# Seven half-width products for two groups of the third block of an attention and SwiGLU kernel

## The chip, the cores and the metric

The kernel runs on one core of one Trainium2 chip. The metric is the device time of one execution in microseconds (us), as the median of several runs. Five engines work side by side: TensorE (PE in the profile) multiplies matrices, VectorE (DVE) and ScalarE (ACT) read its results out of PSUM and do elementwise work, GpSimd (POOL) does elementwise work in SBUF, and SyncE (SP) here issues nearly all DMA transfers. Each engine runs its instructions in order; they wait for each other through semaphores.

## The reference, cut to what matters

```python
# q, k, v: (8, 12, 448, 64); g_q, g_k: (64,)
q_n, k_n = (rmsnorm(q, g_q), rmsnorm(k, g_k))
scores = scale * np.matmul(q_n, k_n.transpose(0, 1, 3, 2))
attn = softmax(scores)                       # over the keys
x = np.matmul(attn, v)                       # -> (3584, 768) tokens by features
g = x @ w_gate                               # (768, 1536), float64 weights
val = x @ w_val
out = (silu(g) * val) @ w_out                # (1536, 768)
```

All results are float32.

## The kernel before, in words

The 8 sequences are worked on in four blocks of two (`block(n)`, n = 0 to 3; in words the first to the fourth). A block has an **up phase** (`x @ w_gate`, `x @ w_val` and the gating) and a **down phase** (the product with `w_out`). The attention of the next block's twelve head pairs (`attention(m)`) is woven into the down phase; its first pairs begin before the up phase has ended. The last block has no attention beside it.

The products work on 3 x 3 arrangements of blocks, with 15 sums of blocks on either side and one product for each: the weights are turned once, at the start, into 15 sums and single blocks of 128 x 128 for each piece (`convert`; kept in device memory as `up_sides[g]` and `down_sides`; `UP_SUMS` is the order of the 11 sums, `BLOCKS` that of the four plain blocks), the activations into 15 sums in `xs` (`sides`), and each product is added to running results t0 to t5 and d by ACT and DVE (`UP_READ`). The up phase falls into four **groups** g = 0 to 3 of hidden features. An ordinary group has 15 steps for the gate and 15 for the value, each one product (`up_product`, line L1498) of two matmuls of 128 x 128 by 128 x 448, since the contraction has two chunks c. Its weights come in three pieces of five steps (`up_load`, `load_sides`, line L1448) into a ring `ws` of two entries.

A group can also be computed by **sevens** (`sevens`, line L1752). There the 2 x 2 scheme of gate and value, two chunks and two halves of the 448 tokens is done in seven products of half width (224 columns) instead of eight. It needs four differences of weights and, on the token side, four differences S1 to S4 of halves for each of the 15 sums. POOL makes the latter while group 0's first pass runs (`halves_of`, L1640); one of them overwrites half of `xs` and is undone afterwards (`restore`, L1654). S1, S2 and S4 lie in `hs`, in the attention's `t`/`QT`/`KT` region of the buffer `work`, and in `es` (the ring `e`); the keys `held` keep the attention out of these for as long. The seven products run as four streams: X and Y, and two products later (`LAG`) Z and W. POOL adds the streams' results (L1863, L1881), DVE joins the last parts, ACT applies SiLU (L1901), DVE multiplies (L1905). With sevens in a block, group 0 runs as two passes with the sevens between them (`passes`): gate, then the sevens, then value, then any further ordinary groups. Before the change only the fourth block (n = 3) has such groups: 1, 2 and 3.

The weight differences are made ahead of time by `prepare`, 15 pieces for three groups, a piece for three of the 15 products (index u): SP loads the six operand blocks' rows from `up_sides` (L1941), POOL makes four subtractions (L1955), and SP stores to `up7_g` (L1962). `PREPARE` gives each block its pieces and `PREPARE_PACE` the spacing of their due times. Before the change there are 8 pieces in the second block (n = 1) and 7 in the third (n = 2), in two places in turn (`es` and the end of `work`), and all seven left operands are stored, plain ones among them. In the fourth block each load of a stream (L1707) is then one DMA from `up7`: four matrices for X and Y, in three places in turn, three for Z and W, in two.

The order on every engine is written by a planner (`Order`): each piece of work has an engine, an estimated cost, a due time, a list of pieces it follows and the rings it takes or uses; it is run through once when the program is built, and the instructions are emitted in that order. The rings are named buffers with a fixed number of entries (`BUFS`): `ws` 2, `qk` 4, `e` 4, `t` 2 and so on.

Of the kernel before, what the change touches and what calls it, by code (L numbers as in the profile page):

```python
# [493 lines left out]
def fast(  # L494
# [91 lines left out]
    def take(name, key, shape):  # L586
# [46 lines left out]
    UP_SUMS = (8, 7, 1, 13, 10, 14, 3, 11, 4, 0, 5)  # L633
# [117 lines left out]
    def attention(m):  # L751
# [19 lines left out]
        def load(x, src):  # L771
            def emit():
# [18 lines left out]
                after=[staged.get(PAIRS)],  # L791
# [622 lines left out]
    PREPARE, PREPARE_PACE, up7_done = {1: [(g, u) for g in (1, 2, 3) for u in range(5)][:8], 2: [(g, u) for g in (1, 2, 3) for u in range(5)][8:]}, 16.0, {}  # L1414
# [44 lines left out]
    def block(n):  # L1459
# [15 lines left out]
        def up_product(g, step, x, which, load, key, when, flip, alone):  # L1475
# [117 lines left out]
        def up_load(g, piece, which, when):  # L1593
            key, more = ("ws", (n, g, piece, which)), []
            if which is not None and piece == (0 if which else 2 if len(seven) % 2 == 0 else None):
                key, more = (("qk", (n, g, piece, i)) for i in range(1)), [("qk", (n, g, piece, i)) for i in range(1, 3)]
                key = next(key)
# [11 lines left out]
            users[key] = [key, *more]  # L1609
            last_load[:] = [load]  # L1610
# [58 lines left out]
        def sevens(begin_seven):  # L1669
# [18 lines left out]
            for (k, late), times in sorted(pieces.items(), key=lambda of: of[1][0]):  # L1688
# [4 lines left out]
                else:  # L1693
                    at = (k - count + 2) % 3
                    name = f"xy{at}"
                    base, tile_of = (0, [ws_keys[at]]) if at < 2 else (4 * P, qk_keys)
# [4 lines left out]
                def load(key=key, tile_of=tile_of, late=late, base=base, k=k, opens=opens):  # L1701
# [7 lines left out]
                done = order.add(  # L1709
                    "SP", 0.6, times[0] - 12.0, load,  # L1710
                    after=[*last_load, up7_done[seven[k // 5], k % 5], clusters[EARLY * (n + 1) - 1, "total"]],
                    takes=[key] + tile_of * opens, uses=tile_of * (not opens),
                    moves=[transfer(P, (36 if late else 48) * P)],
                    early=10.0, rank=SIDES_RANK,
                )
                last_load[:] = [done]
# [11 lines left out]
            for when, stream, j, i in steps:  # L1728
# [64 lines left out]
                def tile_at(stream, t, g=g, key_of=key_of):  # L1793
# [4 lines left out]
                    if ends and key_of(stream, t) == qk_keys[-1]:  # L1798
                        return work[:, 0:S]
# [24 lines left out]
                def emit_read(stream=stream, t=t, how=how, x=x, ps=ps, value=value, first=first, tile_at=tile_at, g=g):  # L1824
# [9 lines left out]
                extra = [("wl", (n, g))] if stream == "W" and x == 4 else []  # L1834
                done = order.add(
                    "ACT" if how == COPY else "DVE", (0.36 if stream == "W" else 0.53) if how == COPY else us,
                    when + 0.2, emit_read, after=[last, *before], takes=extra or ([value] if first else []),
                    uses=([value] if value and not first else []) + ([bank_tile] if bank_tile else []), rank=60.0,
# [159 lines left out]
        if n in PREPARE:  # L1998
            prepare()
# [276 lines left out]
```

## Time and profile before

| | |
|---|---|
| median of 3 runs | 1446.1 us (1443.5 to 1447.08) |
| the profiled execution's own time | 1448.08 us |
| its span, first to last instruction | 1446.2 us |
| granted TensorE clock | 0.997 of full speed |
| PE busy | 1412.9 us (98%) |
| DVE, ACT, POOL busy | 927.0 (64%), 612.5 (42%), 581.1 us (40%) |
| up phase of n = 1 | 483.66 to 669.60 us: 185.94 us |
| up phase of n = 2 | 832.11 to 1018.14 us: 186.03 us |
| up phase of n = 3 | 1179.67 to 1347.01 us: 167.34 us |
| DMA | 234.65 MB, mean 162 GB/s |

Times in the trace are counted from the span's start. A row of an engine's timeline or of the chain gives start, duration and the work (engine, line, output and inputs by their names, a count). A group row gives line, engine, operation, names, shapes and count, then busy time and mean duration, then the idle time before it with what ended it. A float32 matmul appears as two records of PE, which overlap, so the time of a product is read from the distance between starts and not from the sum of durations. The time of a DMA to its landing counts from its issue. Names in the trace are those of the buffers: `work` holds `qk`, `t`, `QT` and `KT`; `mm` and `at` are the banks of the ordinary products; `st` holds the streams Z and W, among others; `up` is the tensor `up7`.

### The profile page before, as it was taken

What the parts mean: (1) busy time and instruction counts of PE and PEld (TensorE: products, weight loads), DVE (VectorE), ACT (ScalarE), POOL (GpSimd) and SP (SyncE); (2) the same over time, 40 slices, a digit from 0 to 9 for tenths busy, and PEclk for the clock granted to TensorE, in tenths of its full rate; (3) what the DMA queues carried; (4) which work ended last, traced back from release to release, by engine and by line L of the source; (5) the groups of instructions that cost most, each with busy time, mean ns of one, the idle gap of its engine ahead of it and who ended that gap; (6) DMA issues with size and microseconds to landing.
All of it is one profiled execution on the core that took longest, in us unless ns stands there. A gap on an engine that the chain in (4) does not pass through costs nothing.

```text
span 1446.2 us, 20499 instructions
## 1 busy us (share of the span) xinstructions
PE 1412.9 (98%) x7006; PEld 739.1 (51%) x7006; DVE 927.0 (64%) x1566; ACT 612.5 (42%) x1244; POOL 581.1 (40%) x698
## 2 busy tenths in 40 slices
PE   8999999989999999999999999999999999999997
PEld 3455454434444455544444455544444448997553
DVE  5889876887866444346776633355686753777633
ACT  6875444466553221256645222245555412432200
POOL 3756666635453122213444222312244448677000
PEclk9999999999999999999999999999999999999999
DMA  7777989854634666843444467673355354543335
GB/s 197 211 217 263 356 279 292 263 164 92 124 78 97 181 228 219 241 138 91 108 91 103 104 195 257 209 188 91 80 110 111 88 119 154 177 168 110 97 100 101
DMA packets 422182, 234.65 MB, mean 162 GB/s; under 512 B 281396, under 2 KB 399924, under 8 KB 420148
## 3 DMA queue, kind: packets, MB, share of 16 engines
q1 hardware_dynamic: 410800, 231.87, 57.3%
q10 hardware_dynamic: 11140, 1.38, 0.7%
q8 instruction: 57, 0.93, 0.3%
q14 instruction: 57, 0.47, 0.1%
q0 software_dynamic: 128, 0.00, 0.0%
HBM read 177.93 MB, written 55.25 MB: 161 GB/s over the span
## 4 chain that ended last, share of the span: by engine, by line
PE 84%; DMA 4%; DVE 4%; SPq 3%; ACT 2%; issue 1%; POOL 1%; ACTq 0%; POOLq 0%; DVEq 0%
PE mm L2076 21%; PE mm L1498 21%; PE at L1498 19%; PE at L1064 7%; PE st L985 7%; PE st L1752 3%; PE at L1752 2%; PE mm L1752 2%; SPq L783 2%; DMA work<-in_k_dram 2%; PE st L1095 1%; PE mm L1095 1%; DMA out_dram<-spare 1%; ACT es L1000 1%; DMA work<-in_q_dram 1%
## 5 line engine op out<-in xcount | busy, mean ns | idle before, releaser
L1498 PE MATMUL mm<-xs,ws 128*128 128x448 f32 x820 | 340.0, 542 | 0.5 <-POOL sums L1863 0.3
L1498 PE MATMUL at<-xs,ws 128*128 128x448 f32 x720 | 301.3, 541 | 4.7 <-DVE v L1429 3.6
L1498 PEld LDWEIGHTS mm<-xs,ws 128*128 128x128 f32 x820 | 155.9, 191 | 154.7 <-issue 150.9
L1498 PEld LDWEIGHTS at<-xs,ws 128*128 128x128 f32 x720 | 135.7, 190 | 142.4 <-issue 124.0
L2076 PE MATMUL mm<-gt,ws 128*128 128x448 f32 x448 | 175.5, 543 | 0.0
L903 POOL TENSOR_TENSOR work<-work,rr 128x448 f32<-128x448 f32 x72 | 72.5, 1026 | 231.4 <-DVE rr L730 82.4
L985 PE MATMUL st<-work 64*64 64x448 f32 (+1 forms) x1536 | 151.4, 500 | 11.8 <-ACT work L933 4.9
L1000 ACT ACTIVATE es<-st 128x896 f32<-128x896 f32 x129 | 114.3, 914 | 100.7 <-PE at L1064 85.7
L2076 PE MATMUL mm<-hs,ws 128*128 128x448 f32 x384 | 151.4, 545 | 0.0
L1005 POOL TENSOR_TENSOR sums<-es 128x896 f32<-128x896 f32 x36 | 76.5, 2126 | 158.4 <-PE st L1095 83.9
L2076 PEld LDWEIGHTS mm<-gt,ws 128*128 128x128 f32 x448 | 83.6, 190 | 83.0 <-issue 80.8
L1427 DVE TENSOR_TENSOR gt<-gt,mm 128x448 f32<-128x448 f32 x52 | 32.3, 621 | 134.5 <-PE mm L1498 132.7
L2076 PEld LDWEIGHTS mm<-hs,ws 128*128 128x128 f32 x384 | 71.2, 190 | 71.4 <-issue 69.9
L1064 PE MATMUL at<-es,v 64*64 64x448 f32 (+1 forms) x1032 | 106.2, 508 | 0.0
L1575 ACT ACTIVATE st<-gt 128x448 f32<-128x448 f32 x78 | 42.6, 547 | 129.3 <-DVE gt L1431 63.3
L985 PEld LDWEIGHTS st<-work 64*64 64x64 f32 x1536 | 50.5, 132 | 81.7 <-issue 36.6
L1425 ACT COPY gt<-mm 128x448 f32<-128x448 f32 x65 | 34.6, 532 | 122.8 <-PE mm L1498 122.7
L1955 POOL TENSOR_TENSOR es<-es 128x384 f32<-128x384 f32 x32 | 31.2, 998 | 121.7 <-DMA es<-up_sides 121.1
L1005 POOL TENSOR_TENSOR sums<-sums,es 128x896 f32<-128x896 f32 x36 | 75.4, 2094 | 2.8
L1064 PEld LDWEIGHTS at<-es,v 64*64 64x64 f32 (+1 forms) x1032 | 43.9, 133 | 56.6 <-issue 49.4
L1425 ACT COPY v<-at 128x448 f32<-128x448 f32 x74 | 39.4, 532 | 58.2 <-PE at L1498 56.7
L822 ACT ACTIVATE work<-work 128x448 f32<-128x448 f32 (+1 forms) x92 | 52.3, 584 | 22.9 <-DMA work<-in_k_dram 10.3
(263 smaller groups left out, 2144.9 us busy)
## 6 DMA issues: line engine op xcount, KB each, us to landing
ws<-up_sides SPq DMA_DIRECT2D x24, 1024.0 KB, 6.5
ws<-down_sides SPq DMA_DIRECT2D x16, 1024.0 KB, 5.7
ws<-down_sides SPq DMA_DIRECT2D x28, 512.0 KB, 5.0
up<-es SPq DMA_DIRECT2D x8, 1344.0 KB, 8.3
out_dram<-spare SPq DMA_DIRECT2D x168, 56.0 KB, 2.1
up<-work SPq DMA_DIRECT2D x7, 1344.0 KB, 9.2
v<-in_v_dram SPq DMA_DIRECT2D x96, 96.0 KB, 2.6
ws<-up_sides SPq DMA_DIRECT2D x12, 768.0 KB, 5.0
```

The lines of the kernel that those rows point to most:

```text
L822: nc.scalar.activation(tiles["t", m][:, x], of, AF.Square)
L903: nc.gpsimd.tensor_tensor(out=tiles["t", m][:, x], in0=tiles["qk", (m, x)], in1=rr.to_broadcast([P, NC, C]), op=ALU.mult,)
L985: nc.tensor.matmul(st[ds(D * x, D), h, 0:n], tiles["KT", m][rows, ds(P * j + D * of_keys, D)], tiles["QT", m][rows, ds(Q * of_queries, n)] ...
L1000: nc.scalar.activation(e, tiles["st", (m, j)][:, :, 0 : S * width(j) // P], AF.Exp)
L1005: nc.gpsimd.tensor_tensor(out=to, in0=tiles["e", (m, 0)] if j == 1 else to, in1=e, op=ALU.add)
L1064: nc.tensor.matmul(tiles["at", (m, x)][ds(D * h, D), ds(0, Q) if early else queries], tiles["v", m][rows, j, h], tiles["e", (m, j)][rows, ...
L1425: nc.scalar.copy(to, ps)
L1427: nc.vector.tensor_tensor(out=to, in0=old, in1=ps, op=ALU.add)
L1498: nc.tensor.matmul(ps(), w[:, 0 if alone else which, c, at], xs[:, SLOT[x], c], start=fresh and c == 0, stop=c == NC2 - 1, skip_group_chec ...
L1575: nc.scalar.activation(take(*act, [P, 2, TB])[:, 0, 0:S], to, AF.Silu)
L1752: nc.tensor.matmul(half(ps(), side), w[:, slot, at], part_of(of, x), start=fresh and side == 0, stop=True, skip_group_check=True,)
L2076: nc.tensor.matmul(banks[bank_of[s]][:, 0:S], w[:, s, g, at], where[x][:, g], start=fresh and i == 0, stop=i == NG - 1, skip_group_check=True,
```

## The change

Groups 1 and 2 of the third block (n = 2) are computed by sevens too, between group 0's two passes; group 3 follows there as an ordinary group.

All 15 pieces of differences are made in the second block (n = 1), due every 7.8 us instead of 16, in three places in turn: `es`, the end of `work`, and group 3's part of `gt`. That group's first results in n = 1 wait until the last piece there is stored (`gt_free`). Only the four differences of a piece are stored; the plain blocks are read from `up_sides` where they are needed, so a load for X and Y is one plain matrix and three differences and one for Z and W two plain ones and one difference, each as two or three DMAs. `prepare` is called ahead of the passes instead of behind them.

In the ring `qk`, a piece of group 0's first pass takes all four entries where the number of groups by sevens is even; the second pass's first piece takes three, and a fourth entry is taken by an empty piece ("places"), which the loads of the next block's q and k follow. These weights and those of the third X and Y place now begin at the start of `work`. In `UP_SUMS`, 4 and 11 change places.

```diff
-    UP_SUMS = (8, 7, 1, 13, 10, 14, 3, 11, 4, 0, 5)
+    UP_SUMS = (8, 7, 1, 13, 10, 14, 3, 4, 11, 0, 5)
...
-    SEVEN = {3: (1, 2, 3)}
+    SEVEN = {2: (1, 2), 3: (1, 2, 3)}
...
-        g: dram.tile([P, 5, 7, 3, P], F32, name=f"up7_{g}")
+        g: dram.tile([P, 5, 4, 3, P], F32, name=f"up7_{g}")
...
-                after=[staged.get(PAIRS)],
+                after=[staged.get(PAIRS), clusters.get("places")],
...
-    PREPARE, PREPARE_PACE, up7_done = {1: [...][:8], 2: [...][8:]}, 16.0, {}
+    PREPARE, PREPARE_PACE, up7_done = {1: [(g, u) for g in (1, 2, 3) for u in range(5)]}, 7.8, {}
...
-            tiles[key] = work[:, 4 * P :]
+            tiles[key] = work[:, 0 : 12 * P]
...
+            if which == 0 and (how == COPY or result == 2) and g == NG - 1:
+                before = gt_free
...
-                key, more = (("qk", (n, g, piece, i)) for i in range(1)), [("qk", (n, g, piece, i)) for i in range(1, 3)]
-                key = next(key)
+                key, *more = (("qk", (n, g, piece, i)) for i in range(3 if which else 4))
...
+            if more and which and n < NB - 1:
+                clusters["places"] = add(
+                    "SP", 0.0, when + 8.0, lambda: None, after=[load], takes=[("qk", (n, "rest", 0))],
+                )
...
-                    src = up7[seven[k // 5]][:, k % 5, 4:7] if late else up7[seven[k // 5]][:, k % 5, 0:4]
-                    nc.sync.dma_start(tiles[key], src.rearrange("p w x f -> p (w x f)"))
+                    first, plain = int(not late), 2 if late else 1
+                    here_of, i = up_sides[seven[k // 5]][:, 0:plain, int(late)], 0
...
+                            nc.sync.dma_start(
+                                w[:, 0:plain, ds(i * P, size * P)],
+                                here_of[:, :, ds(begin + here[0], size)].rearrange("p a x f -> p a (x f)"),
+                            )
...
+                    src = up7[seven[k // 5]][:, k % 5, 3:4] if late else up7[seven[k // 5]][:, k % 5, 0:3]
+                    nc.sync.dma_start(
+                        w[:, 2:3] if late else w[:, 1:4], src.rearrange("p w x f -> p w (x f)")
+                    )
...
-                    after=[*last_load, up7_done[seven[k // 5], k % 5], clusters[EARLY * (n + 1) - 1, "total"]],
+                    after=[last_load[0 if len(loads) > 4 else -1], up7_done[seven[k // 5], k % 5], clusters[EARLY * (n + 1) - 1, "total"]],
...
-            buffers = [(flat_es, ("e",)), (work[:, 2 * NJ * 2 * D * 2 :], ("t", "QT"))]
+            buffers = [
+                (flat_es, ("e",)), (work[:, 2 * NJ * 2 * D * 2 :], ("t", "QT")),
+                (gt[:, NG - 1].rearrange("p k t -> p (k t)"), ()),
+            ]
...
-                which = j % 2
+                which = (j + 1) % 3
...
-                for i, (to, one, two) in enumerate(((2, 1, 0), (3, 5, 2), (1, 5, 1), (6, 4, 3))):
+                for i, (to, one, two) in enumerate(((2, 1, 0), (3, 5, 2), (1, 5, 1), (4, 4, 3))):
...
-                        up7[g][:, u].rearrange("p w x f -> p (w x f)"), raw.rearrange("p w f -> p (w f)")
+                        up7[g][:, u].rearrange("p w x f -> p (w x f)"), raw[:, 1:5].rearrange("p w f -> p (w f)")
...
+            gt_free[:] = [emptied[2]]
+
+        gt_free = [None]
+        if n in PREPARE:
+            prepare()
         passes = [(g, (0, 1)) for g in range(NG) if g not in seven]
...
-        if n in PREPARE:
-            prepare()
```

More of the change, by code (lines that the diff above doesn't have):

```diff
@@ L1705, in load @@
                     tiles[key] = room[:, base : base + (9 if late else 12) * P]
-                    src = up7[seven[k // 5]][:, k % 5, 4:7] if late else up7[seven[k // 5]][:, k % 5, 0:4]
-                    nc.sync.dma_start(tiles[key], src.rearrange("p w x f -> p (w x f)"))
+                    w = tiles[key].rearrange("p (w f) -> p w f", f=3 * P)
+                    first, plain = int(not late), 2 if late else 1
+                    here_of, i = up_sides[seven[k // 5]][:, 0:plain, int(late)], 0
+                    part = UP_ORDER[3 * (k % 5) :][:3]
+                    for names, begin in ((UP_SUMS, 0), (BLOCKS, len(UP_SUMS))):
+                        here = sorted(names.index(x) for x in part if x in names)
+                        if here:
+                            size = len(here)
+                            nc.sync.dma_start(
+                                w[:, 0:plain, ds(i * P, size * P)],
+                                here_of[:, :, ds(begin + here[0], size)].rearrange("p a x f -> p a (x f)"),
+                            )
+                            i += size
+                    src = up7[seven[k // 5]][:, k % 5, 3:4] if late else up7[seven[k // 5]][:, k % 5, 0:3]
+                    nc.sync.dma_start(
+                        w[:, 2:3] if late else w[:, 1:4], src.rearrange("p w x f -> p w (x f)")
+                    )
                 done = order.add(
-                    "SP", 0.6, times[0] - 12.0, load,
-                    after=[*last_load, up7_done[seven[k // 5], k % 5], clusters[EARLY * (n + 1) - 1, "total"]],
+                    "SP", 1.4, times[0] - 12.0, load,
+                    after=[last_load[0 if len(loads) > 4 else -1], up7_done[seven[k // 5], k % 5], clusters[EARLY * (n + 1) - 1, "total"]],
                     takes=[key] + tile_of * opens, uses=tile_of * (not opens),
-                    moves=[transfer(P, (36 if late else 48) * P)],
+                    moves=[
+                        *(transfer((2 if late else 1) * P, 4 * P * i) for i in groups(UP_ORDER[3 * (k % 5) :][:3], UP_SUMS)),
+                        transfer(P, (12 if late else 36) * P),
+                    ],
                     early=10.0, rank=SIDES_RANK,
                 )
-                last_load[:] = [done]
+                last_load[:] = [last_load[-1], done]
                 loads[k, late] = done, key, tile_of
@@ L1834, in sevens @@
                 extra = [("wl", (n, g))] if stream == "W" and x == 4 else []
+                also = held[0:4] if extra else []
                 done = order.add(
@@ L1837, in sevens @@
                     when + 0.2, emit_read, after=[last, *before], takes=extra or ([value] if first else []),
-                    uses=([value] if value and not first else []) + ([bank_tile] if bank_tile else []), rank=60.0,
+                    uses=also + ([value] if value and not first else []) + ([bank_tile] if bank_tile else []), rank=60.0,
                 )
@@ L1895, in sevens @@
                     done = order.add(
-                        "DVE", 0.35, when + 3.0, top, after=[done, ready7[g, result][1]], uses=[ky, *(extra or [kw])], port=True, early=0.0, rank=20.0,
+                        "DVE", 0.35, when + 3.0, top, after=[done, ready7[g, result][1]], uses=[ky, *(extra or [kw]), *also], port=True, early=0.0, rank=20.0,
                     )
@@ L1931, in prepare, with load @@
                 at_first[which] = False
-                def load(four=four, part=part, g=g):
+                def load(raw=raw, part=part, g=g):
                     i = 0
@@ L1962, in prepare @@
                     lambda raw=raw, g=g, u=u: nc.sync.dma_start(
-                        up7[g][:, u].rearrange("p w x f -> p (w x f)"), raw.rearrange("p w f -> p (w f)")
+                        up7[g][:, u].rearrange("p w x f -> p (w x f)"), raw[:, 1:5].rearrange("p w f -> p (w f)")
                     ),
-                    after=[done], uses=keys[which], moves=[transfer(P, 84 * P)], early=0.0,
+                    after=[done], uses=keys[which], moves=[transfer(P, 48 * P)], early=0.0,
                 )
+            gt_free[:] = [emptied[2]]
+        gt_free = [None]
+        if n in PREPARE:
+            prepare()
         passes = [(g, (0, 1)) for g in range(NG) if g not in seven]
```

14 lines of the change are left out of this document (6 added, 8 removed).

## The prediction

> **What bounds the kernel now.** First the head of the page, then the busy time by stretches, then the chain of work that ended last, and last the queue of DMA issues, because that is what the change moves. Blocks are counted n = 0 to 3 as in the code.
>
> ```profile
> span 1446.2 us, 20499 instructions
> PE 1412.9 (98%) x7006; PEld 739.1 (51%) x7006; DVE 927.0 (64%) x1566; ACT 612.5 (42%) x1244; POOL 581.1 (40%) x698
> ```
>
> TensorE (PE) bounds the kernel: it is busy for 98% of the span. The two stretches that the change touches most are the up phases of n = 1 and n = 2; the columns are each engine's busy time, then granted clock, DMA share and GB/s.
>
> ```profile
> 483.66:669.60 185.94, 185.46 (x533) 92.13 (x535) 80.17 (x138) 60.38 (x117) 41.38 (x40) 1.00 0.64 193
> 832.11:1018.14 186.03, 185.54 (x529) 92.31 (x529) 82.44 (x145) 64.47 (x123) 39.32 (x38) 1.00 0.63 183
> 483.66:606.00 122.34, 122.34 (x327) 61.78 (x326) 43.25 (x72) 27.56 (x50) 27.37 (x28) 1.00 0.71 222
> ```
>
> PE is busy for all but half a microsecond of each, at clock 1.00; DVE, ACT and POOL are under half. So fewer PE instructions shorten a block if, and only if, nothing else comes late.
>
> **Groups 1 and 2 of n = 2: the gain.** The chain in n = 2 (start, duration, work; x4 is one product, two matmuls of two records each):
>
> ```profile
> 832.11 1.50 PE mm L1498 x4
> ...
> 952.38 1.50 PE mm L1498 x4
> ...
> 1018.14 3.01 PE mm L2076 x8
> ```
>
> Between the first two rows lie 80 products: 120.27/80 = 1.503 us, so an ordinary group of 30 takes 45.10 us. n = 3 already runs three groups with seven half-width products:
>
> ```profile
> 1179.67 22.55 PE mm L1498 x60
> 1202.22 0.76 PE mm L1752 x4
> ...
> 1240.52 0.76 PE mm L1752 x4
> ...
> 1269.65 0.76 PE mm L1752 x4
> ...
> 1347.01 75.18 PE mm L2076 x200
> ```
>
> From 1240.52 to 1269.65 eleven matrices of the product scheme pass: 29.13/11 = 2.648 us each, 39.72 us for a group's fifteen. Each group saves 45.10 - 39.72 = 5.38 us, both 10.76 us.
>
> **What the form itself costs.** The up phase of n = 3 is 1347.01 - 1179.67 = 167.34 us; group 0 and three such groups make 45.10 + 3 x 39.72 = 164.26. So 3.1 us are lost. Rows of PE in order of time, with the wait in brackets:
>
> ```profile
> 1238.39 0.62 PE L1752 MATMUL at<-hs,ws 128*128 128x224 f32 x2 [0.16 <-DVE spare L1431]
> ...
> 1320.80 1.02 PE L1752 MATMUL st<-xs,ws 128*128 128x224 f32 x4 [0.34 <-DVE gt L1431]
> ...
> 1322.54 1.02 PE L1752 MATMUL st<-xs,ws 128*128 128x224 f32 x4 [0.34 <-DVE gt L1431]
> 1323.78 6.55 PE L1498 MATMUL mm<-xs,work 128*128 128x448 f32 x17
> ```
>
> The first row is a small wait at a change of group, the next two the two lagging streams Z and W, which at the end stand alone and wait for DVE to empty their bank; from 1323.78 to 1347.01, group 0's second pass takes 23.23 us instead of 22.55. With two groups one inner boundary is gone. I take +2.5 us, between +1.9 (the end, 1.2, and the second pass, 0.7) and +4.0.
>
> In n = 2 other work stands behind: group 3 runs last as an ordinary group, 45 us of PE that hide the sums, gates and the 15 POOL restorations, which n = 3 must finish within one half pass. The 60 POOL half differences (0.66 us each) are hidden as in n = 3, where POOL begins them 0.8 us after the block:
>
> ```profile
> 1180.50 0.91 POOL L1640 TENSOR_TENSOR xs<-xs 128x224 f32<-128x224 f32 x1 [12.05 <-PE mm L1498]
> ...
> 1219.73 0.66 POOL L1640 TENSOR_TENSOR es<-xs,work 128x224 f32<-128x224 f32 x1
> ```
>
> They end at 1220.4, and the last is wanted at about 1202.2 + 14 x 2.65 = 1239: 19 us of room. No cost.
>
> **Making the differences, all in n = 1.** Before, 8 preparations lie in n = 1 and 7 in n = 2, one every 16 us; after, 15 in n = 1, one every 7.8 us, in three places. Each is two to four SP loads (768 KB), four POOL subtractions and one SP store, now 768 KB instead of 1344. SP's order in n = 1, and landing times (KB each, median us) of that block:
>
> ```profile
> 498.73 1.19 SPq L1448 DMA_DIRECT2D ws<-up_sides  x2
> 502.17 0.36 SPq L1962 DMA_DIRECT2D up<-es  x1
> ...
> 513.76 1.19 SPq L1448 DMA_DIRECT2D ws<-up_sides  x2
> ...
> 515.71 4.66 SPq L1941 DMA_DIRECT2D es<-up_sides  x4
> ...
> ws<-up_sides SPq DMA_DIRECT2D x7, 1024.0 KB, 6.5
> up<-es SPq DMA_DIRECT2D x4, 1344.0 KB, 7.7
> ```
>
> The landing of all loads of line L1448, and POOL's subtractions (ns, least, median, most):
>
> ```profile
> DMA to landing us min/median/max: 3.4/5.7/8.5
> ...
> L1955 POOL TENSOR_TENSOR es<-es x32: 994/998/1003, 498.2 to 939.8; 128x384 f32<-128x384 f32 x32
> ```
>
> POOL: 28 more subtractions of 1.0 us, on an engine busy 27 of 122 us: no cost. SP and the DMA engines are the question. A weight load (L1448) is issued the moment its ring entry comes free, every 15.03 us, and is wanted 15.03 us later; it lands after 6.5, so it may be 8.5 us late. In the stretch 483.66 to 606.00 the DMA moved 222 GB/s x 122.3 us = 27.2 MB at a share of 0.71. Added: 7 loads of 0.79 MB, and 15 stores of 0.79 in place of about 7 of 1.38, together 7.7 MB; 34.9 MB at the same cost for a MB make a share of 0.91. So transfers will queue, but not grow without end. Low bound: 0 (PE was busy 122.34 of 122.34, there is nothing to win). High bound: a weight load stands behind one preparation's issues (4.7 + 0.4) and one more load's transfer (0.79 MB at 222/0.71 GB/s, 2.5), then lands in 8.5, the longest of line L1448: 16.1 us, 1.1 late, for eight loads 8.6 us. I take +1.0: the median landing with all three delays, 14.1 us, is still in time.
>
> The third place is group 3's part of gt, so that group's first reads wait (gt_free) for the last store there, the 14th of 15. Even at the rate of busy DMA engines alone the 34.9 MB take 34.9/0.313 = 112 us, and the reads are due at 3 x 45.1 = 135: some 20 us of cover, no cost. If it goes, ACT's copies wait there, with all of ACT's queue behind, and PE for its bank.
>
> In n = 2 the seven preparations go. SP, POOL and DMA are relieved, but PE waited for none of them: nothing.
>
> **Loads of the groups of seven.** One DMA a load becomes two or three: plain blocks from up_sides in short rows, differences from up7. The bytes are the same. Streams Z and W have two places, so a load has three matrices, 7.94 us, from free to wanted. In n = 3 now:
>
> ```profile
> ws<-up SPq DMA_DIRECT2D x15, 576.0 KB, 4.0
> ...
> ws<-up_sides SPq DMA_DIRECT2D x2, 256.0 KB, 3.6
> ...
> ws<-up_sides SPq DMA_DIRECT2D x2, 128.0 KB, 3.7
> ```
>
> Three parts issued about 0.5 us apart land in about 4.0 + 1.0 = 5.0 us, inside 7.94; X and Y have three places and twice the room. I take 0. A load that landed as late as the longest weight load above (8.5 + 1.0) would be 1.6 us late; two or three such make 4 us, the high bound, and with nothing to win the low one is 0.
>
> The rule that speaks against this is in "DMA: Bandwidth & Descriptors" of the Trainium skill: its section "Anatomy of one DMA" gives each DMA (measured there for DMAs issued by GpSimd) a fixed part of about 2.0 us, and "Rules for kernel authors" tells one to coalesce small transfers. Taken one after another, two more fixed parts would make an estimated 4.0 + 4.0 = 8.0 us against 7.94, 0.1 us late for each of 25 loads, about +2 us by that page, and the sum -4.6. This trace agrees with a fixed part (128 KB lands in 3.7 us, no sooner than 256 KB in 3.6), and shows for the pairs now issued together that it is not paid one after the other.
>
> **The end of n = 2.** The next attention pairs use the rings (qk, t, QT, KT, e) that the seven products now hold. Now:
>
> ```profile
> 924.36 5.93 SPq L783 DMA_DIRECT2D work<-in_q_dram  x4
> ...
> 938.61 3.54 SPq L783 DMA_DIRECT2D work<-in_k_dram  x4
> ...
> 954.03 2.22 POOL L903 TENSOR_TENSOR work<-work,rr 128x448 f32<-128x448 f32 x2 [13.25 <-DMA work<-in_k_dram]
> ...
> 985.58 1.36 PE L985 MATMUL st<-work 64*64 64x224 f32 x16
> ```
>
> The first q load is issued 92 us after the block's start. After the change, the entries come free with the first five products of group 0's second pass: 22.55 + 79.4 + 2 + 7.5 = 112 us. From the k load to the end of the scaling it is 17.6 us now, so about 135, and the first scores, 32.6 us before the block's end now, would come at about 145. There is some 10 us of cover, and the wait named "places" only keeps the ring's order. Bounds: 0, and 3.6 for two score waits like the one now in the chain (0.98 + 0.96 us of scores take from 1000.67 to 1004.41, 1.8 lost):
>
> ```profile
> 1000.67 0.96 PE st L985 x8
> 1001.65 1.74 ACT es L1000 x2
> ...
> 1003.43 0.98 PE st L985 x8
> 1004.41 1.70 PE at L1498 x4
> ```
>
> I take +0.7. The swap of 4 and 11 in UP_SUMS moves two blocks and adds no instruction: 0.
>
> **The sum.** -10.76 + 2.5 + 1.0 + 0 + 0.7 = -6.6 us. The profiled execution took 1448.1, so 1441.5 against it; it lies 2.0 above the median of the runs, 1446.1, so the median should be 1439.5. With every cost at its low bound: 1446.1 - 10.76 + 1.9 = 1437.2; 1435.3 if the overhead vanished too.
>
> **Rivals.** (1) Queueing in n = 1 makes weight loads late: the slower side. PE would show waits at L1498 for ws<-up_sides between 500 and 610. For it: share 0.91; against it: 8.5 us of room, and stores almost halved. It decides against the change once each of eight loads is over 0.95 us late (10.76 - 2.5 - 0.7 = 7.6). At 1.6 us each: 1446.1 - 7.6 + 12.8 = 1451. (2) The attention's start at the end of n = 2 comes late by more than its cover of 10 us, say 5 us of PE waits: 1439.5 + 4.3 = 1444, no measurable change. For it: 20 us later loads; against: the first scores now come 29 us after their scaling has ended (956.25 to 985.58). (3) Loads of Z and W late by 0.15 us, 25 times, 3.8 us: 1443. Against: the small landings above. (4) The form's own cost is mostly the end's bare streams and group 3 hides all of it but 1 us: 1438; within my range.
>
> **Chances.** Forecast (with 4) 0.68, by itself 1435 to 1442; (1) 0.12; (2) 0.13; (3) 0.07. A measurement of this kernel tells about 0.3%, 4.3 us, from no change: faster is under 1441.8. A tenth of the mild cases (2) and (3) stays faster: faster 0.70, same 0.18, slower 0.12. The range, 1434.5 to 1446, leaves out (1) and little else.
>
> **What would show it.** Right: in n = 2, 240 PE records of the ordinary products out and 420 of the seven in, its up phase about 178 us, n = 1's still 186 to 187, no PE wait for ws<-up_sides. Wrong: n = 1 above 190; gaps before the first scores of n = 2; waits of PE for work or ws loads between the groups.

## The result, and the profile after

| | before | after |
|---|---|---|
| median beside the prediction's runs | 1446.59 us (1443.5 to 1450.86, 4 runs) | 1437.66 us (1437.22 to 1437.9, 4 runs) |
| ratio, with its 95% interval | | 0.9936 [0.991, 0.9962] |
| median in the larger set | 1445.42 us (1443.37 to 1447.88, 17 runs) | 1438.73 us (1437.19 to 1442.36, 6 runs) |
| ratio there | | 0.996 [0.9948, 0.9973] |
| the profiled execution, and its span | 1448.08, 1446.2 us | 1437.9, 1436.1 us |

The changed kernel is 8.9 us faster in the first set and 6.7 us in the larger one, where the forecast was 6.6. Line numbers of the changed kernel are some twenty higher in the middle of the file: the sevens' products are at L1775 and `prepare` has L1967 (loads), L1981 (subtractions) and L1988 (stores).

The head of the profile after:

```profile
span 1436.1 us, 21339 instructions
PE 1402.5 (98%) x7186; PEld 772.0 (54%) x7186; DVE 955.6 (67%) x1621; ACT 618.1 (43%) x1266; POOL 673.9 (47%) x830
```

PE still bounds the kernel, with 180 more records (240 out, 420 in) and 10.4 us less busy time. Now the stretches of the changed kernel, with the columns as before (busy time of PE, PEld, DVE, ACT and POOL, then clock, DMA share, GB/s): the up phases of n = 1, 2 and 3, and the start of the first of them.

```profile
480.60:669.53 188.93, 186.14 (x529) 92.23 (x529) 81.79 (x144) 61.93 (x121) 71.60 (x70) 1.00 0.74 225
831.79:1009.81 178.02, 176.40 (x710) 125.52 (x709) 110.84 (x195) 69.69 (x143) 103.19 (x140) 1.00 0.53 143
1171.22:1338.53 167.31, 166.15 (x752) 141.17 (x751) 110.95 (x189) 51.41 (x107) 116.87 (x162) 1.00 0.50 153
480.60:600.00 119.40, 119.40 (x319) 60.30 (x319) 43.10 (x71) 27.03 (x49) 51.41 (x52) 1.00 0.84 269
```

- n = 2 takes 178.02 us instead of 186.03: 8.0 gained.
- n = 3 takes 167.31 instead of 167.34: the loads in two or three DMAs cost nothing.
- n = 1 takes 188.93 instead of 185.94: 3.0 lost. PE's busy time grew only from 185.46 to 186.14, so PE stands idle there for 2.8 us instead of 0.5. In the first 119 us it does not idle at all, at a DMA share of 0.84; the loss lies behind them.

The rest of the 10.1 us between these two spans lies outside the up phases of n = 1 to 3: 3.1 us ahead of n = 1, 0.4 in the down phases, 1.6 in the tail after the last product. Of the 3.1, 1.65 is a stretch at half clock (last section), and the rest lies ahead of the first block's products (0.9) and in its down phase (0.5). The change touches nothing in the tail. It takes 7.4 to 7.8 us in all thirteen profiled executions of the changed kernel and its variants; of the kernel before there is only this one trace, with 9.0, so it stays open whether that difference is the change's.

In n = 1, PE's waits, from the view of the waits of the changed kernel (us in total, times, longest):

```profile
PE at L1498 <- DVE v L1429: 1.6, 1, 1.6
PE st L985 <- ACT es L1000: 0.5, 2, 0.3
PE at L1498 <- DVE v L1427: 0.5, 1, 0.5
PE at L1498 <- DVE v L1431: 0.3, 1, 0.3
```

None is for `ws<-up_sides`. PE waits for DVE to empty a PSUM bank. The chain of work of the changed kernel at the longest of them shows why DVE was late (start, duration, work):

```profile
610.25 5.92 DMA work<-in_k_dram
...
616.20 0.58 ACT work L822
616.77 0.45 ACT st L1577
...
617.24 0.62 DVE gt L1580
617.87 0.53 DVE gt L1429
618.39 0.54 DVE hs L1204
618.93 0.54 DVE v L1429
...
619.51 1.77 PE at L1498 x4
```

Read it upwards; `...` stands for steps of under 0.1 us. PE's product at 619.51 waits for a read of its bank by DVE, which is queued behind the gating (L1580), which needs ACT's SiLU (L1577), and that stands in ACT's queue behind a square of the next attention (L822), which waits for a load of k. ACT's timeline has the squares of the next attention's first two pairs, with the wait of this one in the last brackets:

```profile
603.52 1.04 ACT L822 ACTIVATE work<-work 128x448 f32<-128x448 f32 x2 [2.08 <-DMA es<-up_sides]
...
607.87 0.58 ACT L822 ACTIVATE work<-work 128x448 f32<-128x448 f32 x1 [2.87 <-DMA work<-in_q_dram]
...
616.20 0.58 ACT L822 ACTIVATE work<-work 128x448 f32<-128x448 f32 x1 [4.22 <-DMA work<-in_k_dram]
616.68 0.53 ACT L1577 ACTIVATE st<-gt 128x448 f32<-128x448 f32 x1
```

The first row begins 123 us into the block. Its squares are written to the ring `t` in `work`, which one of the three places of the preparations overlaps; the last store out of that place landed at 603.37, 0.15 us ahead of them, so this landing fits the wait better than the transfer that the bracket names. Before, the first of these squares came 137 us into the block, 1.6 us after the same store had landed (619.31), and waited for nothing:

```profile
620.93 0.58 ACT L822 ACTIVATE work<-work 128x448 f32<-128x448 f32 x1
```

At the end of the sevens in n = 2, PE's timeline of the changed kernel has the same two waits of Z and W that n = 3 showed before, and then group 0's second pass:

```profile
932.77 1.02 PE L1775 MATMUL st<-xs,ws 128*128 128x224 f32 x4 [0.34 <-DVE gt L1431]
934.52 1.02 PE L1775 MATMUL st<-xs,ws 128*128 128x224 f32 x4 [0.34 <-DVE gt L1431]
935.76 8.06 PE L1498 MATMUL mm<-xs,work 128*128 128x448 f32 x20
```

The sevens run from 831.79 + 22.55 = 854.34 to 935.76: 81.4 us for two groups whose products alone take 79.4.

### The profile page after: what moved, and what is told of

The parts are those of the page before. It is cut to its first block, busy times and chain, and to the rows that moved or that the text cites. A ratio compares the mean times of both kernels' runs of the same rounds, so it can differ in the third digit from the quotient of the medians.

```text
span 1436.1 us, 21339 instructions
## 1 busy us (share of the span) xinstructions
PE 1402.5 (98%) x7186; PEld 772.0 (54%) x7186; DVE 955.6 (67%) x1621; ACT 618.1 (43%) x1266; POOL 673.9 (47%) x830
## 4 chain that ended last, share of the span: by engine, by line
PE 79%; DMA 7%; DVE 4%; SPq 3%; POOL 3%; ACT 2%; issue 2%; POOLq 0%; ACTq 0%; DVEq 0%
PE mm L2104 23%; PE mm L1498 15%; PE at L1498 11%; PE at L1064 8%; PE st L985 7%; PE st L1775 5%; PE at L1775 4%; PE mm L1775 3%; DMA work<-in_k_dram 2%; SPq L783 2%; PE st L1095 1%; PE mm L1095 1%; ACT es L1000 1%; DMA out_dram<-spare 1%; DMA es<-up_sides 1%
## 5 line engine op out<-in xcount | busy, mean ns | idle before, releaser
L1498 PE MATMUL mm<-xs,ws 128*128 128x448 f32 x720 | 293.8, 540 | 0.6 <-POOL sums L1887 0.3
L1498 PE MATMUL at<-xs,ws 128*128 128x448 f32 x540 | 226.4, 542 | 6.9 <-DVE v L1429 5.1
L1498 PEld LDWEIGHTS mm<-xs,ws 128*128 128x128 f32 x720 | 136.3, 190 | 136.1 <-issue 131.3
L1498 PEld LDWEIGHTS at<-xs,ws 128*128 128x128 f32 x540 | 101.4, 190 | 111.9 <-issue 91.5
L1427 DVE TENSOR_TENSOR gt<-gt,mm 128x448 f32<-128x448 f32 x44 | 27.3, 620 | 92.1 <-PE mm L1498 90.4
L1577 ACT ACTIVATE st<-gt 128x448 f32<-128x448 f32 x66 | 35.8, 546 | 101.2 <-DVE gt L1431 39.0
L1425 ACT COPY v<-mm 128x448 f32<-128x448 f32 x60 | 31.9, 532 | 97.2 <-PE mm L2104 55.1
L1775 PE MATMUL st<-xs,ws 128*128 128x224 f32 x300 | 69.7, 355 | 1.4 <-DVE gt L1431 1.4
L1425 ACT COPY gt<-mm 128x448 f32<-128x448 f32 x55 | 29.2, 532 | 95.0 <-PE mm L1498 95.0
L822 ACT ACTIVATE work<-work 128x448 f32<-128x448 f32 (+1 forms) x92 | 51.9, 583 | 30.3 <-DMA work<-in_k_dram 14.7
```

The costliest lines, as they stand in the source:

```text
L822: nc.scalar.activation(tiles["t", m][:, x], of, AF.Square)
L1425: nc.scalar.copy(to, ps)
L1498: nc.tensor.matmul(ps(), w[:, 0 if alone else which, c, at], xs[:, SLOT[x], c], start=fresh and c == 0, stop=c == NC2 - 1, skip_group_chec ...
L1577: nc.scalar.activation(take(*act, [P, 2, TB])[:, 0, 0:S], to, AF.Silu)
L1775: nc.tensor.matmul(half(ps(), side), w[:, slot, at], part_of(of, x), start=fresh and side == 0, stop=True, skip_group_check=True,)
```

## The experiments

All are edits of the changed kernel. "Phases" are the up phases of n = 0, 1, 2, 3 in the profiled execution. Before they were 196.1, 185.9, 186.0, 167.3; after, 194.4, 188.9, 178.0, 167.3.

| run | median us (range, runs) | before beside it | ratio [95%] | phases |
|---|---|---|---|---|
| the change again | 1438.73 (1437.19-1442.36, 6) | 1445.42 | 0.996 [0.9948, 0.9973] | 194.5, 190.1, 178.0, 167.3 |
| e1, no sevens in n = 2 | 1446.83 (1444.78-1450.85, 11) | 1445.42 | 1.0011 [1.0001, 1.0021] | 197.5, 189.8, 185.3, 168.4 |
| e3, supply split | 1450.09 (1446.59-1453.81, 5) | 1445.42 | 1.0039 [1.0026, 1.0052] | 194.4, 189.2, 186.1, 168.3 |
| e4, q and k early | 1440.1 (1438.11-1442.98, 5) | 1445.42 | 0.9959 [0.9946, 0.9972] | 196.1, 190.9, 177.9, 167.4 |
| e5, squares on POOL | 1436.82 (1434.7-1441.0, 6) | 1445.91 | 0.9949 [0.9932, 0.9966] | 194.5, 187.5, 178.0, 167.3 |
| e8, `t` freed early | 1440.39 (1437.03-1446.26, 12) | 1445.91 | 0.9965 [0.9951, 0.9979] | 194.5, 189.3, 178.2, 168.3 |
| e11, pace 7.0 | 1438.11 (1435.94-1438.62, 6) | 1445.91 | 0.9952 [0.9939, 0.9966] | 194.4, 186.5, 178.1, 167.3 |
| e13, e4 and e8 | 1440.24 (1437.94-1445.67, 9) | 1445.91 | 0.997 [0.9956, 0.9984] | 197.7, 189.8, 178.0, 167.3 |
| e12, pace 8.6 | 1437.62 (1435.53-1441.24, 6) | 1445.74 | 0.9952 [0.9934, 0.9969] | 194.4, 187.9, 177.9, 167.3 |
| e14, pace 7.0, squares on POOL | 1438.95 (1435.96-1443.23, 12) | 1445.74 | 0.9958 [0.9946, 0.9969] | 194.1, 189.2, 178.4, 167.3 |
| e15, e14 and first scores later | 1436.92 (1433.24-1440.37, 6) | 1445.74 | 0.9939 [0.9921, 0.9956] | 193.3, 188.2, 178.4, 168.3 |
| e17, pace 7.0 and first scores later | 1440.4 (1437.52-1444.66, 10) | 1446.36 | 0.9959 [0.9947, 0.9971] | 191.7, 191.7, 177.9, 168.3 |

Some of these phases hold stretches of 3.41 us at half clock (last section): n = 0 of before, e4, e11, e14 and e15 one each, n = 0 of e1 and e13 two each, n = 1 of e4 and of e17 one, and n = 2 of e3 one. The two profiled executions of the change, with the same orders on all engines, differ by 1.2 us in n = 1, so differences of that size between single executions tell nothing.

### The change again, and its two halves

> The changed kernel once more beside the kernel before, as the control of this set. If the 8.9 us are the change's own, the ratio is again 0.993 to 0.995 and the up phase of n = 1 about 189 us, of n = 2 about 178 us. If part of the difference was a slow start and a slow end of the kernel before (its trace lost 3.1 us before n = 1 and 1.6 after the last store, where the change does nothing), the difference shrinks to 5 to 6 us, ratio 0.996.

The repeated change gave 1438.73 us against 1445.42, ratio 0.996, as the second alternative has it. The supply alone, without the sevens in n = 2:

```diff
-    SEVEN = {2: (1, 2), 3: (1, 2, 3)}
+    SEVEN = {3: (1, 2, 3)}
```

> The changed kernel with n = 2 of four ordinary groups again; everything else stays: all differences made in n = 1, differences alone stored, the new loads in n = 3. It isolates the price of the supply. By the trace of the change: n = 1 takes 189 us, n = 2 186 or a little less, n = 3 167.3; total 3 us above the kernel before where the start is equal, ratio 1.002. By the prediction's sizes (supply +1.0): ratio 1.001. If the supply costs nothing and the 189 us belonged to that one execution: ratio 1.000 or below.

It is 1.4 us above before (0.1 to 3.0 by its interval), and the sevens, put back, bring 1446.83 - 1438.73 = 8.1. The two add up to the total by construction; what parts them is the phases. n = 1 took 189.8 us here too: what it loses belongs to the supply, not to the sevens. That is 3.9 us more than before in this one phase, where the medians tell of 1.4 for the whole kernel.

### Is it the crowd of transfers in n = 1?

Two things set the loads of q and k of that stretch: SP and the DMA engines busy with the preparations (theory 1), or the place in `work` that one of the three preparation places shares with the ring `t`, which comes free only with its last store (theory 2). First, five of fifteen pieces moved back to n = 2, all of those through `gt`:

```diff
-    PREPARE, PREPARE_PACE, up7_done = {1: [(g, u) for g in (1, 2, 3) for u in range(5)]}, 7.8, {}
+    PREPARE, PREPARE_PACE, up7_done = {1: [(g, u) for g in (1, 2) for u in range(5)], 2: [(3, u) for u in range(5)]}, {1: 11.7, 2: 16.0}, {}
...
-                which = (j + 1) % 3
+                which = (j + 1) % 3 if n == 1 else 2
```

> The changed kernel with the differences of group 3, which only n = 3 uses, made in n = 2 in group 3's part of gt alone, and ten instead of fifteen pieces in n = 1, due every 11.7 us. Theory 1 (the crowding of n = 1's DMA queue makes the k load late, ACT waits for it and PE for ACT and DVE): n = 1 falls from 189 to about 186 us, n = 2 stays within 1 us of 178, total 2 to 3 us under the change. Rival (POOL and SP are already full in n = 2 with the half differences): n = 2 rises by as much as n = 1 falls, no gain.

n = 1 did not recover with a third fewer pieces (189.2 us), although the DMA share in its first 119 us fell from 0.84 to 0.70. So the loss does not need the crowd. The run does not test the place, since the last store out of `work` was issued 6 us later in the block than in the change. And n = 2 lost all that the sevens bring, 1.65 of it to a stretch at half clock. Its stretch, and POOL's waits in it:

```profile
831.48:1017.58 186.10, 178.84 (x709) 126.79 (x709) 112.42 (x195) 70.15 (x143) 123.66 (x160) 0.99 0.62 179
```

```profile
POOL gt L1981 <- DMA gt<-up_sides: 8.9, 3, 3.6
```

POOL stood 8.9 us, in order, before the preparations' subtractions, with the block's own sums behind them, and PE idled 7.3 us in n = 2. Of PE's two long waits there, the chain of one (2.78 us) runs over those sums on POOL (L1887); the chain of the other (3.03 us) goes back over DVE alone. So it does matter that all differences are made in n = 1. That POOL, at 124 of 186 us, has time in n = 2 for the work but not for the waiting is shown for the first of these waits and likely for the rest.

Next, the loads themselves 16 us earlier:

```diff
-                "ACT" if both else "SP", 0.5 if natural else 1.4 if both else 2.4, ready - 28.0, emit, takes=[("qk", (m, x))],
+                "ACT" if both else "SP", 0.5 if natural else 1.4 if both else 2.4, ready - (44.0 if m in (24, 25) else 28.0), emit, takes=[("qk", (m, x))],
```

> The changed kernel with the loads of q and k of the first two pairs woven into n = 1's end (24 and 25) due 16 us earlier. Theory 1 (ACT stands behind the late k load): the ACT wait of 4.2 us for k at 612 us goes, and with it PE's 1.6 us wait; n = 1 at 186 to 187 us, total 2 us under the change. Rival (it is the amount of traffic, whatever waits for it): the loads only displace weight loads or preparations, another wait takes its place, n = 1 stays near 189.

n = 1 took 190.9 us. Of these, some 1.65 are from a stretch at half clock (613.75 to 617.16) right behind PE's wait of 2.07; the rest, about 189.2, is no better than the change. ACT's square now waited, and longer, for the last store out of `work`; SP issued that store at 604.44, some 3.5 us later in the block than in the change:

```profile
608.65 1.98 ACT L822 ACTIVATE work<-work 128x448 f32<-128x448 f32 x4 [5.37 <-DMA up<-work]
```

The load of k by itself was not the cause, and theory 1 fell in that form. The time is what the rival had: the earlier loads displaced preparations, and another wait took the place of the first.

### The queue on ACT

If ACT's order is the link, taking those squares off ACT must help though nothing on SP or PE moves. Only the engine of the squares of two pairs is changed:

```diff
-    SQUARED = (2, 3)
+    SQUARED = (2, 3, 24, 25)
```

> The changed kernel with the squares of pairs 24 and 25 (the first woven into n = 1's end) made by POOL instead of ACT; the orders of PE and SP stay the same. Theory 2 (in n = 1 ACT's squares stand ahead of its SiLU instructions, and wait for the last store out of the work region and for the late k load; the gates behind them come late, then DVE, then PE's bank): the PE gaps of 1.0, 2.4 and about 1 us near 610, 618 and 645 us of the changed kernel lose the first two, n = 1 falls from 189 to 190 us to about 186.5, total 2.5 to 3 us under the change. Rival (crowded DMA: what waits is weights): n = 1 stays at 189 or above.

In the two executions of the change, PE waits for DVE near 611 us (0.3 and 0.5 us), 619 (1.6 and 1.8) and 645 (0.5 and 1.2). Here the first two are gone, and n = 1 takes 187.5 us; 186.5 was expected. PE's and SP's instructions stand in the order that they have in the change, and the last store out of `work` and the late k load are issued at the same times (599.3 and 607.3 us, against 599.1 and 607.2). So the supply was as late as before, and only its way to PE was cut. One wait is left, from the next pair, whose squares stayed on ACT: the stretch, PE's wait, and ACT's.

```profile
480.35:667.82 187.47, 185.76 (x529) 92.32 (x529) 82.44 (x144) 60.04 (x117) 75.57 (x74) 1.00 0.75 227
```

```profile
PE at L1498 <- DVE v L1427: 1.2, 1, 1.2
```

```profile
641.79 0.58 ACT L822 ACTIVATE work<-work 128x448 f32<-128x448 f32 x1 [1.49 <-DMA work<-in_k_dram]
```

The same link tested from the supply's side: the preparations closer together, so more crowded, but done earlier.

```diff
-    PREPARE, PREPARE_PACE, up7_done = {1: [(g, u) for g in (1, 2, 3) for u in range(5)]}, 7.8, {}
+    PREPARE, PREPARE_PACE, up7_done = {1: [(g, u) for g in (1, 2, 3) for u in range(5)]}, 7.0, {}
```

> The changed kernel with a piece of differences due every 7.0 us instead of 7.8. It ends about 11 us earlier by the due times, and crowds the DMA queue more while it lasts. Theory 2: the last store out of the work region comes earlier by up to 9 us and the loads of q and k find an emptier queue: n = 1 falls by 1 to 3 us. Rival (crowding itself costs): n = 1 rises above 189 us, with PE waits for ws<-up_sides between 490 and 590 us.

n = 1 falls to 186.5 us, nearly to the 185.9 of before. By the rival, crowding would have made it worse. The square that waited 2.87 us for q in the change waits for nothing, and of PE's waits for DVE one of 0.4 us is left:

```profile
604.56 0.58 ACT L822 ACTIVATE work<-work 128x448 f32<-128x448 f32 x1
```

The end of `work`'s pieces can also come sooner by their order alone, with the last three in `gt`, `es`, `gt`:

```diff
-                which = (j + 1) % 3
+                which = (j + 1) % 3 if j < 12 else (2, 0, 2)[j - 12]
```

> The changed kernel with the last three pieces of differences placed in gt, es, gt instead of work, gt, es, so that the work region (the ring t, which the squares need) is empty one turn earlier. Theory 2: the planner sets the squares earlier; the wait for the store goes, the one for late k loads may stay: n = 1 at 187 to 189 us. If the ring alone were the cause: 186. Rival (crowding): no change, 189 or more, since the same bytes move at the same pace.

The planner, seeing the place free, put the squares earlier, and they then waited for the loads: 189.3 us.

```profile
598.29 0.58 ACT L822 ACTIVATE work<-work 128x448 f32<-128x448 f32 x1 [4.06 <-DMA work<-in_k_dram]
```

This edit of `which` and that of `ready` in e4 together:

> Both the placement of the last three pieces (gt, es, gt) and the loads of q and k of pairs 24 and 25 due 16 us earlier. Each takes away one of the two things that ACT's squares wait for. Theory 2: here both are gone, n = 1 at 186 to 187 us, total 2.5 to 3 us under the change, although each alone helps little. Rival (crowding): 189 or more.

This missed what theory 2 expected: n = 1 takes 189.8 us. The place came free earlier, but the planner set the first squares earlier still, and they wait until the last store out of `work` has landed (586.99); PE waits 1.63 us behind them. Then pair 26's squares wait for q, and PE 2.02 us behind those:

```profile
587.16 0.58 ACT L822 ACTIVATE work<-work 128x448 f32<-128x448 f32 x1 [3.62 <-DMA es<-up_sides]
...
624.41 0.58 ACT L822 ACTIVATE work<-work 128x448 f32<-128x448 f32 x1 [3.37 <-DMA work<-in_q_dram]
```

### Pace the other way, and the fixes together

Pace 8.6 instead of 7.8:

```diff
-    PREPARE, PREPARE_PACE, up7_done = {1: ...}, 7.8, {}
+    PREPARE, PREPARE_PACE, up7_done = {1: ...}, 8.6, {}
```

> The changed kernel with a piece of differences due every 8.6 us instead of 7.8: less crowding, later end. Theory 2: the last store out of the work region comes up to 10 us later, into the middle of the first pairs' squares; ACT waits longer or the pairs start late: n = 1 at 189 us or above, up to 3 us more. Crowding as the cause: n = 1 falls towards 186 us.

ACT waits longer for the last store, but at fewer places, and n = 1 takes 187.9 us; neither expectation was met. Both 7.0 and 8.6 give a shorter n = 1 than 7.8, so neither less crowding nor an earlier end orders the results by itself.

```profile
614.50 0.58 ACT L822 ACTIVATE work<-work 128x448 f32<-128x448 f32 x1 [4.89 <-DMA up<-work]
```

Pace 7.0 with the squares of pairs 24, 25 and 26 on POOL:

```diff
-    SQUARED = (2, 3)
+    SQUARED = (2, 3, 24, 25, 26)
...
-    PREPARE, PREPARE_PACE, up7_done = {1: ...}, 7.8, {}
+    PREPARE, PREPARE_PACE, up7_done = {1: ...}, 7.0, {}
```

> Both remedies: due every 7.0 us, and the squares of pairs 24, 25 and 26 on POOL. With pace 7.0 alone n = 1 took 186.5 us, with POOL's squares alone 187.5, of which 1.0 us was the same kind of wait at pair 26. Theory 2: together 186 us, total 3 us under the change (1435 to 1436). If the two remedies meet in POOL (squares behind subtractions that wait for their loads): n = 1 at 187 us or above.

The two helps don't add: 189.2 us, the time of the second alternative. A new wait runs past ACT, over POOL's squares into DVE's queue, and PE waits 3.1 us, as the chain of that kernel shows:

```profile
591.85 7.27 DMA es<-up_sides
599.11 0.93 POOL work L820
...
600.06 1.09 DVE ss L853
601.15 0.54 DVE v L1427
...
601.73 1.77 PE at L1498 x4
```

POOL's timeline has the wait of the first square. The subtractions stand behind it, not ahead of it, and the last store out of `work` landed at 597.99, so it is the place in `work` again, now on POOL:

```profile
598.21 1.82 POOL L820 TENSOR_TENSOR work<-work 128x448 f32<-128x448 f32 x2 [8.59 <-DMA es<-up_sides]
```

Two runs moved the first block's first scores, because of two waits of PE of 2.6 us near 293 and 304 us: on top of e14 (e15), and on top of pace 7.0 alone (e17).

```diff
-            when = (ready + 0.3 + (13 if m == EARLY else 0.0) if j in (3, 0) else base) + 0.01 * (j % 3)
+            when = (ready + 0.3 + (18 if m == EARLY else 0.0) if j in (3, 0) else base) + 0.01 * (j % 3)
```

> As the kernel before in this call (pace 7.0, POOL's squares), and the first scores of the second attention, pair 12 at the end of n = 0, due 18 instead of 13 us after their base. At that place every kernel so far has two PE waits of 2.6 us, and in some executions the granted clock is 0.5 for 3.41 us right behind one of them, 1.7 us each time. If the waits bring the half clock: the up phase of n = 0 falls from 194.4 us by 2 us or more, no half clock there, and the runs lie closer together. If PE waits there for something that the later due time does not move: 194.4 us stay and the half clock goes on appearing in some runs.

> The candidate: the changed kernel with a piece of differences due every 7.0 us (squares on ACT as in the change) and the first scores of pair 12 due 18 instead of 13 us after their base. From the runs so far: n = 1's up phase 186.5 us as with pace 7.0 alone, n = 0's about 191.7 us without a half clock (193.3 with one), so 2.5 us and 2.7 us under the change, a median of about 1434 and a lowest run of 1431 to 1432. If, as with both remedies together, the shifted orders bring another wait in n = 1, n = 1 is at 188 to 189 us again and the median 1436.

In both, the second wait is gone and the first, 2.56 us, stays. In e15 a stretch at half clock follows it, so n = 0 falls by only 1.1 us, to 193.3; n = 1 takes 188.2. In e17 there is none in n = 0, and the shift takes 2.7 us out of it. But the order that it shifts brings them back in n = 1 (191.7 us): ACT's square waits 6.55 us for the load of k, PE 3.4 for DVE, and a stretch at half clock right behind (600.57 to 603.98, PE busy for 2.96 of it) adds some 1.5.

```profile
598.69 0.58 ACT L822 ACTIVATE work<-work 128x448 f32<-128x448 f32 x1 [6.55 <-DMA work<-in_k_dram]
```

No variant is clearly better than the change. e5 and e15 have the lowest medians, and their intervals overlap that of the repeated change.

## Why the prediction was right, and where it was off

**The gain and the form's cost: right.** In one set, n = 2 takes 185.3 us without the sevens (e1) and 178.0 with them: 7.3 us, where 10.76 - 2.5 - 0.7 = 7.6 was forecast; the medians of the two give 8.1. The sevens themselves lose 81.4 - 79.4 = 2.0 us, and by the two profiled phases all other costs in n = 2 come to 10.76 - 8.0 - 2.0 = 0.8, where the forecast had 2.5 and 0.7. Rival 4, that group 3 hides all but 1 us of it, did not happen: both end waits stand there unchanged.

**Loads in two or three DMAs: right at 0.** In n = 3 of the changed kernel the plain pairs and the differences land like this (KB, median us):

```profile
ws<-up SPq DMA_DIRECT2D x15, 192.0 KB, 3.7
...
ws<-up_sides SPq DMA_DIRECT2D x14, 256.0 KB, 3.2
ws<-up_sides SPq DMA_DIRECT2D x22, 128.0 KB, 2.9
```

The phase of n = 3 didn't move by 0.1 us, so rival 3 fell. Fixed costs paid one after the other, which the prediction worked out from the Trainium skill's "DMA: Bandwidth & Descriptors" ("Anatomy of one DMA") as an estimate of about +2 us, did not show. The trace does not agree with that reading, for DMAs issued by SP.

**The end of n = 2: right.** The first q load is issued at 941.96, 110 us into the block (forecast 112), and the first scores start at 977.25, 145 us into it (forecast 145):

```profile
941.96 1.90 SPq L783 DMA_DIRECT2D work<-in_q_dram  x4
...
977.25 1.36 PE L985 MATMUL st<-work 64*64 64x224 f32 x16
```

PE waits for nothing between; what remains of its waits in this block is small (the view of the waits, changed kernel, n = 2), and rival 2 did not happen:

```profile
PE st L1775 <- DVE gt L1431: 0.7, 2, 0.3
PE st L985 <- ACT es L1000: 0.5, 2, 0.3
...
```

**The supply in n = 1: the step that failed.** The prediction looked for its cost in late weight loads (rival 1), took +1.0, and wrote that n = 1 would stay at 186 to 187. It took 188.9 and 190.1 us in the two profiled executions: 3 to 4 us in the phase. e1's median put the supply at 1.4 us, with an interval that reaches 3.0; its n = 2, without preparations, is 0.7 shorter than before, where the prediction had nothing. The DMA share came to 0.84, not 0.91, and the weight loads were in time. The price was paid at a place that the prediction had not listed among those who wait: it followed SP's queue to the weight loads and to `gt_free`, but not to the next attention's q and k loads and their squares, whose place `t` in `work` the preparations use, and from there into ACT's queue. The place shows in ten of the thirteen profiled executions of the changed kernel and its variants: the first of these squares begins 0.07 to 0.24 us after the last store out of `work` has landed, after 2.0 to 9.0 us of idle on its engine. e5 shows the link to PE, with the orders of PE and SP unchanged: the wait goes over ACT's squares to DVE and to PE's bank. e4, e8, e13, e14 and e17 show that it is not one late transfer: each of these edits leaves or brings squares, of the same or of other pairs, that stand ahead of their place or their data. Why the planner, whose estimated landing times order these queues, comes out well at pace 7.0 and not at 7.8 was not settled further. And in the medians neither e5 nor e11 is told apart from the change, so the link is shown in the trace of the phase and not in the time of the kernel.

**The sum: near, and in part by luck.** By medians of one set the supply costs 1.4 (forecast 1.0) and the sevens bring 8.1 (forecast 7.6), so two misses of half a microsecond cancel, and the total is -6.7 against the forecast -6.6. More than that cancels. All terms of the sum lie in the up phases of n = 1, 2 and 3, and these together are 5.0 us shorter than before's in one profiled execution of the change and 3.9 in the other. The other 1.6 to 2.8 us of the median's 6.7 would then come from elsewhere, where the prediction had nothing: in these traces the start, n = 0's phases and the tail are shorter than in the one trace of before, and only n = 0's half clock has a known reason. The first set's -8.9 owes 1.2 us to before's higher median there and 1.1 to the change's lower one; its four executions of the change have clocks of 0.998 and 0.999, the larger set's six 0.996 to 0.999, so fewer stretches at half clock are likely part of it.

**The swap in `UP_SUMS`: right at 0.** n = 0 takes 194.4 us after; before it takes 196.1 with one half-clock stretch of 1.65, which leaves 194.4, and e4, the changed order with one stretch at the same place, takes 196.1 too.

**Open:** n = 3 took 168.3 to 168.4 us instead of 167.3 in e1, e3, e8, e15 and e17. In each, PE stands 0.98 us in group 0's second pass, where the change stands 0.27 (for POOL's sums), and the profile shows nothing that it waits for; no run gives the reason.

## What to carry to other kernels

An added stream of transfers need not be paid first by the loads that look tightest. Here it was paid by an engine whose in-order queue held an instruction that needed a delayed transfer, or a place that one had to free, ahead of work that the bounding engine needed. So list those neighbours for every ring and place that the stream uses, not only its queue. Where a planner orders the queues by estimated landing times, a shift of due times can move such a wait elsewhere, so a fix at one place need not be worth its own size. And a total that comes out as forecast is no proof of its terms: compare each term with its own phase, as here 3 to 4 us lost in n = 1 against a forecast of 1.0.

## What the runs showed of the hardware that was not expected

Behind the same wait of PE, the clock drops in some executions and not in others, and the traces show what decides. At 293 us both kernels have this wait (PE's timeline, before and then after):

```profile
296.04 1.00 PE L985 MATMUL st<-work 64*64 64x448 f32 x8 [2.56 <-ACT work L940]
296.98 3.35 PE L1498 MATMUL mm<-xs,ws 128*128 128x448 f32 x4
```

```profile
295.12 0.98 PE L985 MATMUL st<-work 64*64 64x448 f32 x8 [2.56 <-ACT work L940]
296.04 1.77 PE L1498 MATMUL mm<-xs,ws 128*128 128x448 f32 x4
```

The product behind it takes 3.35 us before and 1.77 after. In each of the 14 traces, every change of the granted clock falls a whole number of steps of 3.413 us after the moment at which the trace first has full clock: before, that moment is 6.74 us, and the drop at 296.87 comes 85 steps later. So PE's idle time can be counted step by step. Before, the wait lies whole within one step, and the next step has half the clock (PE's busy time is the number behind the length, the clock the third from the right):

```profile
293.46:296.87 3.41, 0.85 (x9) 0.21 (x8) 2.30 (x7) 2.39 (x8) 0.34 (x1) 1.00 1.03 367
296.87:300.28 3.41, 3.41 (x12) 1.20 (x8) 0.80 (x2) 0.92 (x1) 1.84 (x2) 0.50 0.84 197
```

After, the same wait is split between two steps, 1.00 and 1.56 us, and the clock stays:

```profile
290.15:293.57 3.42, 2.41 (x7) 0.95 (x5) 2.04 (x6) 1.77 (x5) 2.47 (x4) 1.00 1.01 332
293.57:296.98 3.41, 1.85 (x11) 0.78 (x12) 1.43 (x6) 2.38 (x7) 0.73 (x1) 1.00 1.04 378
```

Over all steps of the 14 traces that end before the last product does, this comes out as one line: behind each of the eleven steps in which PE idled 2.00 us or more (up to 3.03), the clock was halved; of three steps with 1.97 or 1.98 us one was followed by half clock; of all others, with 1.95 or less, none. So whether a wait of 2.56 us brings the half clock goes by how it falls on these steps, and that is chance: they stand differently to the kernel's start in each execution (the first full clock came between 5.2 and 7.6 us).

A half-clock stretch lasts 3.41 us and costs up to 1.65. The block has two waits of that size, and n = 0 took 194.4 us with none of the stretches, 196.1 with one and 197.5 or 197.7 with two (before, after, e1, e4, e13). But e11 and e14, with the same orders in n = 0 and one stretch, took 194.4 and 194.1, as their second wait shrank from 2.56 to 0.58 and 0.31 us. This is part of the 3 to 9 us by which runs of one kernel differ in the larger sets, so a difference of a single profiled pair is to be read block by block. The Trainium skill, "TensorE: Matmul & The Clock Gate", Part 1, gives the gate a free-running window of about 3.4 us and halves the clock after an idle window. The trace agrees on the length and on a grid that does not start with the kernel; but here a window that was idle for 2.00 of its 3.41 us was enough.
